# A chunked linear-attention layer and its MLP: v of the first three units loaded once and re-ordered by products, weights converted in five steps

## The chip, the cores and the metric

The kernel runs on one core of one Trainium2 chip. The metric is the device time of one execution in microseconds (us), as the median of several runs. Beside it there is one execution taken with the hardware profiler, whose span and rows are used below; it has a time of its own.

## The reference: what is computed

An attention block with a decaying state is followed by an MLP on its output.

```python
# B, H, S, D = 4, 8, 768, 48; q, k, v, f_logit are float32
f = 1 / (1 + exp(-f_logit))
state = zeros(B, H, D, D)
for t in range(S):
    state = f[:, :, t, :, None] * state + einsum('bhd,bhe->bhde', k[:, :, t], v[:, :, t])
    y[:, :, t] = einsum('bhd,bhde->bhe', q[:, :, t], state)
x = y.transpose(0, 2, 1, 3).reshape(3072, 384)
h = x @ w_in                          # w_in: 384 x 2048
g = h / (1 + exp(-1.702 * h))
out = g @ w_out                       # w_out: 2048 x 384
```

The two weight matrices arrive as float64 (6.3 MB each). The kernel reads them as pairs of 32-bit words and makes float32 of them itself.

## The kernel before, in words

**Units.** The 4 x 768 tokens are cut into 12 units of 256 tokens (three for each batch), numbered n = 0 to 11. A unit has an attention part, `attention(n)`, and an MLP part over its 256 rows. The first three units (`N_FILL = 3`) differ from the others in how q, k and f are brought in: they are loaded token-major (`load_raw`, L235) and turned by products with an identity matrix (`turn`, L311), copied out of PSUM by ScalarE (L314).

**Attention of a unit.** Within blocks of 64 tokens the work goes by levels m = 1, 2, 4, 8, 16, 32. At each level a "score" product `sc` (L349) is formed from the k of the first half and the q of the second half of each pair of blocks of m tokens; VectorE multiplies it by a mask (`evacuate`, L373) into A; and `add` (L406) multiplies A into the rows of v and adds into the PSUM tile `y`. Between two levels `promote` multiplies q and k by products of f: k on VectorE (L389), q on GpSimd (L390); ScalarE then copies the first halves of k into `Kc` (L396), which the next level's scores read. The tile `sc` has one buffer, so a level's scores also wait until the mask of the level before is through. After the levels, k is transposed (`tkn`, L467, copied to `kn` by ScalarE, L468), the products of k and v per block (L484) go into the running state `st` on VectorE (L498 to L503), and the state is multiplied into `y` (L519). ScalarE copies `y` out (L528), and DMAs re-arrange it into `xT`, the MLP's input (L530, L537).

**v in seven orders.** `add` needs the rows of v in seven orders: the even and the odd tokens of each pair (`vl` 0 and 1), and for each level m = 2 to 32 the first-half rows (`vl` 2 to 6). All are 128 x 384 tiles. A DMA first writes v of a unit token-major into a DRAM tile (`order_v`, L254: `v_tok`, in runs of 48 floats), then six DMAs read it back, one for orders 0 and 1 together (L267) and five for the others (L272), and a seventh reads it in plain token order (`load_vn`, L278) for L484. Each `vl` and `vn` has one buffer, so the loads for unit n + 1 wait until unit n has used the one before; they are issued at the levels of unit n.

**Weights.** `fetch_weights` (L160) brings the float64 weights as 16 pairs of pieces of 128 x 384; three buffers (`bits`) are in flight. For each piece ScalarE makes a float32 from the upper word (`a`, L188), and VectorE then runs a chain of six operations on 128 x 384 elements: L203 a maximum with a constant (the clamp), L204 shift and flip, L199 sign, L207, L208, L209. The operations of the two pieces of a pair alternate. `convert` issues one of them; `merge` spreads `pieces * NOP` such operations over the parts of a unit (8, 10, 8 and 6 pieces for units 0 to 3; NOP = 6), and MLP products over the same parts.

**Order.** The order of instructions on TensorE (PE) is written out by hand through all units, and on all engines up to unit 3: every engine then runs its list in that order. MLP products are laid in from unit 1 on; which of them may be issued depends on the pieces already converted. The SP queue issues nearly all DMAs in program order: first the q, k, f of unit 0, then weights, `vl` and `vn` of unit 0, then q, k, f of unit 1, and so on; only the first `v_tok` is issued by ScalarE. The program gives its DMAs eight completion counters in turn, so a DMA also waits until the one eight places before it has landed.

Of the kernel before, what the change touches and what calls it, by code (L numbers as in the profile page):

```python
# [23 lines left out]
def kernel(  # L24
# [40 lines left out]
    HS = 64  # L65
    LEV = [1 << i for i in range(C.bit_length() - 1)]
    NL = len(LEV)
# [43 lines left out]
    for l, m in enumerate(LEV):  # L111
        nc.vector.tensor_scalar(masks[:, l, :], at[0], float(m), None, op0=ALU.is_lt)

    F = const.tile([P, NA], F32, name="F")

    X = const.tile([P, 3, NA], F32, name="X")
# [23 lines left out]
                (lambda t: t[:], moe_w_out[ff * P:(ff + 2) * P, :].rearrange("(c p) f -> p c f", c=2))]))  # L140
        pieces += [w_in[:, :, ff * P:(ff + 1) * P] for ff in ffs] + [w_out[:, ff, :] for ff in ffs]
    NPC = 2 * FG
    NOP = 6
    fetched, todo = {}, []
    state = {"fetch": 0, "begin": 0, "done": 0}

# [20 lines left out]
    def begin_pair(m):  # L167

        chains = []
        for n in (2 * m, 2 * m + 1):
            if n not in fetched:
                continue
            dst = pieces[n]
            bits = fetched.pop(n)
            at = (slice(None),) * (len(dst.shape))
            lo, hi = bits[at + (0,)], bits[at + (1,)]

            def tmp(tag, bufs, n=n, dst=dst):  # L180
# [7 lines left out]
            nc.scalar.activation(a, hi.bitcast(F32), AF.Abs, scale=2.0 ** 112)  # L188
            chains.append(chain(dst, lo, hi, a, tmp))
        for ops in zip(*chains):  # L190
            todo.extend(ops)
        todo.append(None)

    def chain(dst, lo, hi, a, tmp):
        ve, ai, t = nc.vector, a.bitcast(I32), {}

        def sign():
            t["s"] = tmp("s", 2)
            ve.scalar_tensor_tensor(  # L199
                t["s"].bitcast(I32), hi, -(1 << 31), ai, op0=ALU.bitwise_and, op1=ALU.bitwise_or  # L200
            )
        return (
            lambda: ve.tensor_scalar(a, a, 2.0 ** 97, None, op0=ALU.max),  # L203
            lambda: ve.tensor_scalar(ai, ai, 3, -(1 << 31), op0=ALU.logical_shift_left, op1=ALU.bitwise_xor),  # L204
            sign,

            lambda: ve.tensor_scalar(ai, t["s"].bitcast(I32), -(1 << 23), None, op0=ALU.bitwise_and),  # L207
            lambda: ve.scalar_tensor_tensor(a, lo.bitcast(U32), 2.0 ** -52, a, op0=ALU.mult, op1=ALU.mult),  # L208
            lambda: ve.tensor_tensor(dst, a, t["s"], ALU.add),  # L209
        )  # L210
# [37 lines left out]

    def order_v(n, engine=nc.sync):

        if n >= NALL:
            return
        b, s0 = n // NU, n % NU * U
        engine.dma_start(  # L254
            out=v_toks[n % 2].rearrange("t (h d) -> t h d", h=H),
            in_=v[b, :, s0:s0 + U, :].rearrange("h t d -> t h d"),
        )

    def load_vl(n, u):


        if n >= NALL:
            return
        v_tok = v_toks[n % 2]
        if u == 0:
            t = ld.tile([P, 2, DM], F32, tag="vl0", name=f"vl_{n}_0")
            nc.sync.dma_start(out=t, in_=v_tok.rearrange("(p two) e -> p two e", two=2))  # L267
            vls[n, 0], vls[n, 1] = t[:, 0], t[:, 1]
        else:
            m, half = V_HALF[u]  # L270
            t = vls[n, u] = ld.tile([P, DM], F32, tag=f"vl{u}", name=f"vl_{n}_{u}")
            nc.sync.dma_start(out=t, in_=v_tok.rearrange("(n two m) e -> two n m e", two=2, m=m)[half])  # L272

    def load_vn(n):
        if n >= NALL:
            return
        vns[n] = ld.tile([P, NG, DM], F32, tag="vn", name=f"vn_{n}")
        nc.sync.dma_start(out=vns[n], in_=v_toks[n % 2].rearrange("(g p) e -> p g e", g=NG))  # L278

    def rows(h):  # L280
# [6 lines left out]
    def attention(n):  # L287
# [155 lines left out]
        def level(l):  # L443
            sc = scores()
            score(sc[:, :, :256].rearrange("p h (a t) -> p h a t", a=NP), keys(l), tokens(1, LEV[l], 1))
            if l == 2:
                add(1, slot(t["A"], 0), half(1, 1))
                add(2, slot(t["A"], 256), half(LEV[1], 1))
                load_vl(n + 1, 0)
                load_vl(n + 1, 2)  # L450
            else:
                add(l, slot(t["A"], 0), half(LEV[l - 1], 1))
                load_vl(n + 1, l)
            promote(l)
            t["A"] = evacuate(256, [(0, l)])

        for l in range(2, NL):
            part("W")(lambda l=l: level(l))
# [14 lines left out]
        @part("W")  # L473
        def _():
            add(NL, slot(t["A"], 0), half(LEV[-1], 1))
            load_vl(n + 1, NL)

            pd = scores()
            for a in range(NP):
                for g in range(NG):  # L480
                    for h in range(2):
                        for c in range(2):
                            x = (a * NG + g) * D
                            nc.tensor.matmul(  # L484
                                pd[h * HS:(h + 1) * HS, c, x:x + D],
                                lhsT=t["kn"][c * C:(c + 1) * C, a, g, h * HS:(h + 1) * HS],
                                rhs=vns[n][c * C:(c + 1) * C, g, (2 * a + h) * D:(2 * a + h + 1) * D],
                                start=True, stop=True,
                            )
            load_vn(n + 1)  # L490
            st = att.tile([P, NC, NP, D], F32, tag="st", name=f"st_{n}", bufs=2)
            D64 = t["tms"][NL].rearrange("p (a c) -> p a c", c=NC)
            prev = last.get("st")
            t["before"] = [prev[:, NC - 1] if c == 0 and not first else st[:, c - 1] if c else None for c in range(NC)]
            for c in range(NC):
                d = pd[:, c % 2, :NP * NG * D].rearrange("p (a g e) -> p a g e", a=NP, g=NG)[:, :, c // 2, :]
                if t["before"][c] is None:
                    nc.vector.tensor_copy(st[:, c], d)  # L498
                    continue
                nc.vector.tensor_tensor(  # L500
                    st[:, c], t["before"][c], D64[:, :, c:c + 1].broadcast_to((P, NP, D)), ALU.mult
                )
                nc.vector.tensor_tensor(st[:, c], st[:, c], d, ALU.add)  # L503
            last["st"] = st
# [80 lines left out]
    def mlp_unit(n):  # L585
        g = {}

        def done(tt, po):
            o = mlp.tile([P, DM], F32, tag="osb", name=f"osb_{n}_{tt}")
# [31 lines left out]
    def parts_of(n):  # L621

        parts = list(units[n][1])
        if n + 1 < NALL:
# [3 lines left out]
            parts.insert(9, ("-", begin_gates))  # L628
            parts.insert(8, ("B", begin_k))
            parts.insert(6, ("B", begin))  # L630
        return parts

    def merge(n, fill, columns, share, pieces=0, hold=0, by=1.0):
# [91 lines left out]
```

## Time and profile before

| | |
|---|---|
| median of 3 runs | 723.3 us (722.66 to 724.5) |
| profiled execution | 726.69 us, its span 724.9 us |
| mean granted TensorE clock | 0.974 |
| PE busy | 684.1 us (94% of the span) |
| VectorE (DVE) busy | 403.0 us (56%) |
| ScalarE (ACT) busy | 198.1 us (27%) |
| GpSimd (POOL) busy | 66.1 us (9%) |
| moved by DMA | 73.20 MB, mean 101 GB/s |

The profile's page gives busy times over the whole span; a matmul counts as busy from its start to its modelled end, so 94% is not 94% of the engine's peak. The span falls into two stages with different limits: the first hundred us or so, in which the weights come in and the first units run without much MLP work, and the long rest. Sums over the span say little about the first stage; it is read from tables by stretches of time, from the waits, and from the instructions in order of time. The 1.8 us between the span and the profiled time lie outside of the profiled instructions.

### The profile page before, as it was taken

How to read it: one execution, taken by the hardware profiler on the slowest of the kernel's cores; microseconds unless marked ns; L12 is line 12 of the kernel's file. 1: busy time of each engine (PE TensorE's matmuls, PEld its weight loads, DVE VectorE, ACT ScalarE, POOL GpSimd, SP SyncE). 2: the span in 40 equal slices, each digit the busy share in tenths (PEclk: the TensorE clock that was granted, in tenths of full speed). 3: DMA queues.
4: the chain of work that ended last, by engine and by line, in shares of the span. 5: the costliest groups of instructions: out<-in, count | busy, mean ns of one | idle time of the engine just before them, and what ended most of it. 6: DMA issues, size and time to landing. Idle time of an engine off the chain costs nothing.

```text
span 724.9 us, 20635 instructions
## 1 busy us (share of the span) xinstructions
PE 684.1 (94%) x9152; PEld 511.6 (71%) x9152; DVE 403.0 (56%) x697; ACT 198.1 (27%) x408; POOL 66.1 (9%) x103
## 2 busy tenths in 40 slices
PE   4567879999999999999999999999999999999998
PEld 4556657677677686686686686686686686686774
DVE  2959876798685753653653653653654654352120
ACT  2332442242222222222222222222222222122120
POOL 3314221210001001001001001001001001000000
PEclk9676999999999999999999999999999999999999
DMA  8879693385126434514513614514513211100000
GB/s 208 197 195 233 181 213 107 99 203 110 56 57 158 126 91 113 142 38 105 144 44 86 162 44 108 137 48 108 141 45 87 67 34 45 35 3 16 29 0 23
DMA packets 69097, 73.20 MB, mean 101 GB/s; under 512 B 30096, under 2 KB 61200, under 8 KB 69008
## 3 DMA queue, kind: packets, MB, share of 16 engines
q1 hardware_dynamic: 66944, 71.49, 38.4%
q8 instruction: 72, 1.18, 0.7%
q10 hardware_dynamic: 2064, 0.39, 0.3%
q14 instruction: 17, 0.14, 0.1%
HBM read 62.42 MB, written 9.44 MB: 99 GB/s over the span
## 4 chain that ended last, share of the span: by engine, by line
PE 86%; DVE 6%; DMA 5%; SPq 1%; issue 1%; ACT 1%; DVEq 0%; ACTq 0%
PE o L573 35%; PE h L557 33%; PE sc L349 6%; PE y L406 6%; PE sc L484 2%; DMA raw<-in_f_logit_dram 1%; PE y L519 1%; DMA v_tok<-in_v_dram 1%; PE tkn L467 1%; DMA bits<-in_moe_w_in_dram 1%; DMA bits<-in_moe_w_out_dram 1%; PE t L311 1%; DVE a L208 1%; DVE s L199 1%; DVE A L373 1%
## 5 line engine op out<-in xcount | busy, mean ns | idle before, releaser
L573 PE MATMUL o<-w_out,g 128*128 128x384 f32 x768 | 266.7, 496 | 2.8 <-DVE g L563 2.8
L557 PE MATMUL h<-xT,w_in 128*128 128x256 f32 x1152 | 264.3, 383 | 0.0
L557 PEld LDWEIGHTS h<-xT,w_in 128*128 128x128 f32 x1152 | 214.3, 190 | 33.3 <-issue 0.8
L573 PEld LDWEIGHTS o<-w_out,g 128*128 128x128 f32 x768 | 142.6, 191 | 94.8 <-issue 5.8
L563 DVE TENSOR_TENSOR g<-h,sg 128x256 f32<-128x256 f32 x192 | 80.9, 423 | 145.5 <-ACT sg L562 144.8
L562 ACT ACTIVATE sg<-h 128x256 f32<-128x256 f32 x192 | 73.5, 384 | 162.7 <-PE h L557 155.4
L396 ACT COPY Kc<-X 128x512 f32<-128x512 f32 x60 | 37.7, 629 | 171.9 <-DVE X L392 126.2
L392 DVE TENSOR_TENSOR X<-X,tot 128x1024 f32<-128x1024 f32 x45 | 54.9, 1219 | 35.2 <-PE sc L349 35.2
L373 DVE TENSOR_TENSOR A<-sc,masks 128x512 f32<-128x512 f32 (+1 forms) x84 | 62.6, 755 | 2.5 <-PE sc L349 2.5
L406 PE MATMUL y<-A,vl 64*48 64x64 f32 (+1 forms) x2688 | 61.9, 234 | 0.0
L406 PEld LDWEIGHTS y<-A,vl 64*48 64x48 f32 x2688 | 52.3, 125 | 5.8 <-issue 5.7
L349 PEld LDWEIGHTS sc<-X,Kc 48*64 48x64 f32 x1920 | 36.3, 142 | 28.2 <-issue 24.6
L338 POOL TENSOR_TENSOR tot<-F 128x512 f32<-128x512 f32 x12 | 12.5, 1041 | 479.2 <-DVE st L500 438.7
L349 PE MATMUL sc<-X,Kc 48*64 48x64 f32 x1920 | 44.1, 232 | 9.8 <-ACT Kc L396 8.1
L528 ACT COPY yT<-y 48x512 f32<-48x512 f32 x48 | 27.8, 580 | 76.1 <-PE y L519 57.9
L299 DVE STREAM_TRANSPOSE X<-raw 128x1024 f32<-128x1024 f32 x18 | 36.8, 2045 | 7.5 <-PE sc L349 7.1
L349 PEld LDWEIGHTS sc<-X 48*64 48x64 f32 x768 | 19.2, 144 | 22.9 <-issue 15.6
L349 PE MATMUL sc<-X 48*64 48x128 f32 (+1 forms) x768 | 24.0, 265 | 11.5 <-DVE A L373 5.6
L343 DVE TENSOR_TENSOR X<-X,F 128x1024 f32<-128x1024 f32 x12 | 14.7, 1223 | 25.3 <-PE y L519 15.5
L390 POOL TENSOR_TENSOR X<-X,tot 128x512 f32<-128x512 f32 x15 | 23.4, 1561 | 53.4 <-PE sc L349 53.4
L503 DVE TENSOR_TENSOR st<-st,sc 128x192 f32<-128x192 f32 x44 | 15.6, 354 | 19.9 <-PE sc L484 18.6
L392 DVE TENSOR_TENSOR X<-X,F 128x1024 f32<-128x1024 f32 x9 | 11.0, 1225 | 27.7 <-PE sc L349 27.7
(44 smaller groups left out, 365.0 us busy)
## 6 DMA issues: line engine op xcount, KB each, us to landing
vl<-v_tok SPq DMA_DIRECT2D x60, 192.0 KB
bits<-in_moe_w_out_dram SPq DMA_DIRECT2D x8, 768.0 KB
bits<-in_moe_w_in_dram SPq DMA_DIRECT2D x8, 576.0 KB
vl<-v_tok SPq DMA_DIRECT2D x12, 384.0 KB
vn<-v_tok SPq DMA_DIRECT2D x12, 384.0 KB
v_tok<-in_v_dram SPq DMA_DIRECT2D x11, 384.0 KB
xT<-yT SPq DMA_DIRECT2D x24, 144.0 KB
raw<-in_f_logit_dram SPq DMA_DIRECT2D x18, 192.0 KB
```

The lines of the kernel that those rows point to most:

```text
L299: nc.vector.transpose(out.rearrange("p (a i j) -> p a j i", a=NP, j=R), raw[:, j].rearrange("p a (j d) -> p (a j) d", j=R)[:, :, :32],)
L349: nc.tensor.matmul(out[g * HS:(g + 1) * HS, h, a, :], lhsT=lhs(h, a * U + g * G), rhs=rhs(h, a * U + g * G), start=True, stop=True,)
L373: nc.vector.tensor_tensor(A[:, :, c:c + w].rearrange("p h (x t) -> p h x t", t=64), t["sc"][:, :, c:c + w].rearrange("p h (x t) -> p h x t ...
L390: nc.gpsimd.tensor_tensor(qk[:, 0], qk[:, 0], by[:, 0], ALU.mult)
L392: nc.vector.tensor_tensor(qk, qk, by, ALU.mult)
L396: nc.scalar.copy(Kc.rearrange("p (n m) -> p n m", m=m), X[:, 2].rearrange("p (n two m) -> p n two m", two=2, m=m)[:, :, 0, :],)
L406: nc.tensor.matmul(dst(h, g, a), lhsT=vls[n, u][g * 64:(g + 1) * 64, (2 * a + h) * D:(2 * a + h + 1) * D], rhs=A(h, g, a), start=(start an ...
L528: nc.scalar.copy(yT[rows(h), :, g, :], py[columns(h, g), g])
L557: nc.tensor.matmul(ph, lhsT=w_in[:, c, ff * P:(ff + 1) * P], rhs=xTs[n][:, c, :], start=(c == 0), stop=(c == NK - 1))
L562: nc.scalar.activation(sg, ph, AF.Sigmoid, scale=1.702)
L563: nc.vector.tensor_tensor(g[ff // FG][:, ff % FG, :], ph, sg, ALU.mult)
L573: nc.tensor.matmul(t["po"], lhsT=g[ff // FG][:, ff % FG, tt * P:(tt + 1) * P], rhs=w_out[:, ff, :], start=(ff == ffs[0]), stop=(ff == ffs[ ...
```

## The change

For units 0, 1 and 2, v is loaded once in token order, straight from the input into `vn` (two DMAs of 128 tokens each, in runs of 48 floats); the DRAM tile and its six read-backs fall away for these units. The seven orders are made by products: for each order two products (g = 0, 1), with 64 columns of the identity, or of `perm`, as the stationary operand and the 128 x 384 rows of v as the moving one, fill the two halves of a PSUM tile, and ScalarE copies it to `vl`. `perm` holds identity columns for the levels 2 to 32, made once by five GpSimd copies. The products for unit 0 lie before and among its own first parts; those of unit n + 1 behind each level's `add` in unit n. `vn` of unit 1 takes the buffer of the MLP's output tile. That tile now holds both 128-row halves of a unit and has one buffer; before, each half had one of two.

The conversion of the weights loses the clamp (L203): ScalarE scales by 2 to the power -112 without taking the magnitude, VectorE shifts left by three without the flip, and the rest is as before. NOP goes from 6 to 5.

```diff
-    NOP = 6
+    NOP = 5
...
-            nc.scalar.activation(a, hi.bitcast(F32), AF.Abs, scale=2.0 ** 112)
+            nc.scalar.activation(a, hi.bitcast(F32), AF.Copy, scale=2.0 ** -112)
...
-            lambda: ve.tensor_scalar(a, a, 2.0 ** 97, None, op0=ALU.max),
-            lambda: ve.tensor_scalar(ai, ai, 3, -(1 << 31), op0=ALU.logical_shift_left, op1=ALU.bitwise_xor),
+            lambda: ve.tensor_scalar(ai, ai, 3, None, op0=ALU.logical_shift_left),
...
+    perm = const.tile([P, NL - 1, 64], F32, name="perm")
+    for u in range(2, NL + 1):
+        nc.gpsimd.tensor_copy(
+            perm[:, u - 2].rearrange("p (n m) -> p n m", m=LEV[u - 1]),
+            ident.rearrange("p (n two m) -> p two n m", two=2, m=LEV[u - 1])[:, 0],
+        )
...
     def order_v(n, engine=nc.sync):
-        if n >= NALL:
+        if n >= NALL or n < N_FILL:
             return
...
+        if n < N_FILL:
+            for i, x in enumerate((0, 1) if u == 0 else (u,)):
+                pt = ps.tile([P, DM], F32, tag="mm", name=f"tv_{n}_{x}", bufs=4)
+                for g in range(NG):
+                    nc.tensor.matmul(
+                        pt[g * 64:(g + 1) * 64], lhsT=ident[:, x::2] if u == 0 else perm[:, u - 2, :], rhs=vns[n][:, g, :],
+                        start=True, stop=True,
+                    )
+                if i == 0:
+                    t = ld.tile([P, 2, DM] if u == 0 else [P, DM], F32, tag=f"vl{u}", name=f"vl_{n}_{u}")
+                vls[n, x] = t[:, x] if u == 0 else t
+                nc.scalar.copy(vls[n, x], pt)
+            return
...
-        vns[n] = ld.tile([P, NG, DM], F32, tag="vn", name=f"vn_{n}")
+        vns[n] = (mlp if n == 1 else ld).tile([P, NG, DM], F32, tag="osb" if n == 1 else "vn", name=f"vn_{n}", bufs=1)
+        if n < N_FILL:
+            b, s0 = n // NU, n % NU * U
+            for g in range(NG):
+                nc.sync.dma_start(
+                    out=vns[n][:, g].rearrange("p (h d) -> p h d", h=H),
+                    in_=v[b, :, s0 + g * P:s0 + (g + 1) * P, :].rearrange("h p d -> p h d"),
+                )
+            return
...
     for j in range(3):
         load_raw(0, j)
-    order_v(0, nc.scalar)
+    load_vn(0)
     fetch_weights()
...
-    load_vl(0, 2)
-    load_vl(0, 3)
     fetch_weights()
-    for u in range(4, NV):
-        load_vl(0, u)
-    load_vn(0)
     for j in range(3):
         load_raw(1, j)
+    load_vn(1)
```

In the order written out, the products for `vl` 0 and 1 of unit 0 stand between the turning of q, k, f and the first scores; 2 and 3 behind the first scores; 4, 5 and 6 behind the second part's `add`. Those of unit 1 stand in unit 0: 0, 1 and 2 behind the `add` of level 2, then one order behind each `add`, and order 6 behind L484. Those of unit 2 stand in the same way in unit 1.

More of the change, by code (lines that the diff above doesn't have):

```diff
@@ L448, in level, with values @@
                 add(2, slot(t["A"], 256), half(LEV[1], 1))
-                load_vl(n + 1, 0)
-                load_vl(n + 1, 2)
             else:
                 add(l, slot(t["A"], 0), half(LEV[l - 1], 1))
-                load_vl(n + 1, l)
+            if n + 1 >= N_FILL:
+                values(l)
             promote(l)
             t["A"] = evacuate(256, [(0, l)])
+            if n + 1 < N_FILL:
+                values(l)
+        def values(l):
+            for u in (0, 2) if l == 2 else (l,):
+                load_vl(n + 1, u)
         for l in range(2, NL):
@@ L475, in _ @@
             add(NL, slot(t["A"], 0), half(LEV[-1], 1))
-            load_vl(n + 1, NL)
+            if n + 1 >= N_FILL:
+                load_vl(n + 1, NL)
             pd = scores()
@@ L489, in _ @@
                             )
-            load_vn(n + 1)
+            if n + 2 < N_FILL:
+                load_vn(n + 2)
+            if n + 1 >= N_FILL:
+                load_vn(n + 1)
+            else:
+                load_vl(n + 1, NL)
             st = att.tile([P, NC, NP, D], F32, tag="st", name=f"st_{n}", bufs=2)
@@ L588, in done @@
         def done(tt, po):
-            o = mlp.tile([P, DM], F32, tag="osb", name=f"osb_{n}_{tt}")
+            if tt == 0:
+                g["o"] = mlp.tile([P, U // P, DM], F32, tag="osb", name=f"osb_{n}", bufs=1)
+            o = g["o"][:, tt]
             nc.scalar.copy(o, po)
@@ L623, in parts_of @@
         parts = list(units[n][1])
+        if n == 0:
+            parts.insert(2, ("-", lambda: [load_vl(0, u) for u in range(4, NV)]))
+            parts.insert(1, ("-", lambda: [load_vl(0, u) for u in (2, 3)]))
         if n + 1 < NALL:
@@ L627, in parts_of @@
             parts.append((kind, lambda: (fn(), begin_q())))
-            parts.insert(9, ("-", begin_gates))
-            parts.insert(8, ("B", begin_k))
-            parts.insert(6, ("B", begin))
+            i = len(parts)
+            parts.insert(i - 1, ("-", begin_gates))
+            parts.insert(i - 2, ("B", begin_k))
+            parts.insert(i - 4, ("B", begin))
         return parts
```

## The prediction, as it was put on record

> **What bounds the kernel now.** I read the table of busy times by stretches first, since the share over the span hides two stages. Columns: stretch, its length, busy time of PE, PE weight loads, VectorE, ScalarE, GpSimd, granted clock, DMA share, GB/s.
>
> ```profile
> 14.60:36.00 21.40, 11.64 (x416) 10.45 (x416) 19.91 (x37) 5.92 (x12) 7.90 (x8) 0.73 0.86 206
> 36.00:49.80 13.80, 9.81 (x207) 8.94 (x200) 6.41 (x16) 5.33 (x10) 1.59 (x1) 0.87 0.84 212
> ...
> 56.70:80.00 23.30, 17.57 (x406) 14.51 (x410) 22.24 (x49) 6.60 (x15) 8.66 (x5) 0.79 0.85 221
> 80.00:94.00 14.00, 14.00 (x192) 10.54 (x191) 9.32 (x24) 6.90 (x13) 2.68 (x1) 0.90 0.82 187
> 94.00:107.00 13.00, 10.59 (x210) 7.83 (x200) 11.48 (x24) 4.35 (x9) 4.54 (x7) 1.00 0.95 214
> ...
> 155.00:200.00 45.00, 45.00 (x552) 32.29 (x551) 35.06 (x71) 13.32 (x29) 3.54 (x6) 1.00 0.45 108
> ```
>
> From about 110 us on PE is full and everything else is cover; what is gained there must be PE time, and the change gives none. Before that, in unit 0 (14.6 to 56.7) and unit 1 (56.7 to about 103), VectorE is the fullest: 19.9 of 21.4 us, 22.2 of 23.3. So the end moves by the time at which unit 2's dense part begins, and hardly by anything else.
>
> Second, the waits between 32 and 48 us, where VectorE has a hole (6.4 of 13.8 us):
>
> ```profile
> DVE a L203 <- ACT a L188: 5.2, 1, 5.2
> ACT a L188 <- DMA bits<-in_moe_w_out_dram: 4.8, 1, 4.8
> ...
> PE sc L484 <- ACT kn L468: 3.5, 1, 3.5
> ```
>
> ScalarE stood 4.8 us at the head of its list for a pair of weights, with `kn` behind it, and PE waited 3.5 us for `kn`. The SP queue in order of time says why these weights were late (start, length, instruction):
>
> ```profile
> 18.19 0.38 SPq L278 DMA_DIRECT2D vn<-v_tok  x1
> 19.07 4.85 SPq L235 DMA_DIRECT2D raw<-in_f_logit_dram  x4
> 24.62 4.83 SPq L235 DMA_DIRECT2D raw<-in_q_dram  x4
> 29.55 1.77 SPq L235 DMA_DIRECT2D raw<-in_k_dram  x4
> 31.37 0.65 SPq L254 DMA_DIRECT2D v_tok<-in_v_dram  x1
> 36.53 0.35 SPq L267 DMA_DIRECT2D vl<-v_tok  x1
> 36.98 0.57 SPq L272 DMA_DIRECT2D vl<-v_tok  x1
> 37.66 0.53 SPq L160 DMA_DIRECT2D bits<-in_moe_w_out_dram  x1
> ```
>
> Their DMA left at 37.66, behind unit 1's v, though their buffer was free at about 25, when the first pair's last L208 had run (23.69 + 1.02).
>
> **What the Trainium skill says.** "TensorE: Matmul & The Clock Gate", specifications: ScalarE and VectorE take instructions in strict order; the 4.8 us wait above, with `kn` behind it, agrees. Same page, part 3: products on different column groups of the array run side by side. The trace agrees: L311 writes 64 columns each, 64 products of 128 elements take 3.71 us at full clock (84.05), so 116 ns a pair, where one L557 of 256 takes 229 (264.3 us / 1152), so about 115 for 128. Same page, part 1: an idle PE is clocked at half speed until it has been busy some microseconds; the trace has 0.50 from 18 to 24 us and from 50 to 64. "DMA: Bandwidth & Descriptors", specifications: a transfer below 512 B is a read-modify-write. v's runs are 192 B; their cost into SBUF no row of before shows, into DRAM it does (below).
>
> **The change part by part**, against the profiled execution (726.7: span 724.9 and 1.8 outside), 3.4 above the median of 723.3.
>
> *1. Start: -1.3 us.* `v_tok`, at 0.73 beside the first loads, goes, and with it SP's 1.8 us wait for it in the middle of q. f should land about 1.3 earlier than 6.25 (0.39 MB less at 265 GB/s is 1.5). The turning of q, k, f keeps its 7.75 us on PE and ends near 12.7. The four products for `vl` 0 and 1 come next, two pairs of 384 elements: 3 x 116 = 0.35 us a pair warm, 0.48 cold (36 to 38 us: 25 in 2 us). They end at 13.4, about when ScalarE has copied k (12.7 + 0.6), so the first scores start at 13.4 against 14.69. The price rests on v's landing: issued at about 7.5, needed at 12.7. Bounds: `v_tok`'s queue moved 2064 packets in 0.3% of 16 engines' span, 2.2 us; at the mean of the main queue (38.4% x 16 x 724.9 / 66944 = 67 ns a packet) 2048 packets take 8.5; twice that, an estimate from the page's read-modify-write, is 17. I take 3 to 5 with latency.
>
> *2. Levels of unit 0: +0.5.* By level 5 the five-step chain issues 25 operations where the six-step one issued 30 (40 and 48 over 28 shares, 18 of them here). An L203 took 0.44 us (8.8 / 20 before 110 us), the operations left slightly more, so this is worth 4 to 5 x 0.4 = 1.8 where VectorE is the last to come. PE gets 11 pairs. A level has some 1.2 to 2 us in which PE waits for VectorE, GpSimd and `Kc`, which covers one pair, and two behind the first scores (PE idle 15.8 to 19.3). Not covered: orders 4 to 6, three cold pairs, 1.44 us; PE ends `add` at 21.6 and starts the scores at 23.1, where 22.91 was the old time, so the 1.3 and the first savings are gone; and of unit 1's orders 0 to 2 another 0.3. I charge 2.3. v of unit 1 must have landed by 26: SP now issues it at about 20, once the third pair of weights (3.9 MB from 2 us at 260 GB/s, near 17) has freed the counters. The seven ScalarE copies a unit (0.48 each, the duration of L605) are hidden: 5.9 busy of 21.4. The five `perm` copies fall in GpSimd's idle time from 2 to 10.6. Together 2.3 - 1.8 = +0.5, so -0.8 so far; bounds -1.8 and +3.
>
> *3. The wait for weights: -3.5.* The fourth pair is issued as soon as its buffer is free, near 25, and has 16 us to land. ScalarE copies `kn` at about 42, PE goes from `add` (ended 44.36) into L484, not at 47.83. Next late is the PE list itself, full from 36.05 to 44.36, with one pair more (in part 2). Sum -4.3.
>
> *4. Between state and unit 1: -0.4.* VectorE runs four instead of five chain operations (3.3 us from 52.03) before L343. -4.7.
>
> *5. Unit 1 to 84 us: -0.7.* 32 chain operations for 38 save 6 x 0.4 = 2.4. Against it ScalarE: its copies of `vl` stand before the sigmoids (L562) for which VectorE waits in order. At level 2 three copies (1.44) put `sg` at about 70.3 where VectorE gets to it at 69.5: 0.8; at level 3, where it waits 1.06 already, 0.5. From 80 to 94 PE is full: one pair, 0.35 to 0.4. 2.4 - 1.3 - 0.4 = 0.7. -5.4.
>
> *6. From 94 to 109.6: -0.9.* VectorE is the fullest again, and two to three L203 lie on the way to the `g` for which PE waits 2.8 us at 109.63. PE's list has one pair, under the state's 2.8 us. -6.3.
>
> *7. After that: +0.3.* The order of MLP products on PE is the same. The hole at 147.4 (1.63 us, PE behind VectorE) may shrink or grow by an operation; I leave +0.3 for it. Single-buffered output tile: its next user is a unit, some 45 us, later: nothing. Without the `v_tok` chain the weights also come earlier, but after 46 us nobody waited for them: nothing.
>
> Sum -6.0: 720.7 profiled, 717.3 as a median.
>
> **The rivals.**
>
> *A. The forecast, 717.3;* own range 714.8 to 720.5, the bounds of parts 2 and 5.
>
> *B. VectorE all the way.* If PE's pairs and ScalarE's copies are all covered, the 20 L203 before 110 us (8.8) and the hole of 4.8 both come back: 723.3 - 13.6 = 709.7. For it: 93 and 95% busy. Against: at 22.91 and 26.37 the scores already waited on PE's and GpSimd's side.
>
> *C. The pairs take the place of what goes.* 21 pairs at 0.42, the mean of warm and cold, are 8.8 us. If all are on the path in place of the 2.7 charged (2.3 and 0.4), the sum is -6.0 + 6.1: 723.4, no change. For it: PE is in order and every pair stands before scores. Against: PE is idle 9.8 of 21.4 us in unit 0.
>
> *D. Slower: v by token lands late.* With read-modify-write at 17 us, v of unit 0 lands at 24.5 and PE, in order, starts the first scores at 25.2, 10.5 after before. Parts 2 to 7 (-4.7) stay: 723.3 + 5.8 = 729.1. It decides from a landing later than 12.7 + 6 = 18.7 on. For it: 2048 runs of 192 B, ahead of the weights in the same queue. Against: `v_tok` had the same runs, and its first load took 5.2 us in the chain of waits.
>
> That the change doesn't do what it says could only be the ScalarE step: Copy for magnitude. L314 uses Copy already and the page has a single table load, so I give it no price.
>
> **How the numbers follow.** A 0.50, B 0.12, C 0.20, D 0.18. A measurement of this kernel tells 0.3%, 2.2 us, from no change: below 721.1 is faster, above 725.5 slower. A and B are faster (0.62), C is spread over 720 to 726 and gives 0.03 faster, 0.13 same, 0.04 slower; D gives 0.02 same and 0.16 slower. Faster 0.65, same 0.15, slower 0.20. The range of 710.0 to 725.5 leaves out most of D and some of B, about 0.2.
>
> **What would show it right or wrong.** Right: first scores near 13.4; ScalarE's wait for `bits` near 42 gone and L484 near 43.5; unit 1's first scores at 52; PE dense from about 103.5; the rest shifted by the same. Part 2 is wrong if the scores behind orders 4 to 6 start much past 23; part 5 if VectorE waits more than 2.5 us for `sg`. D shows as PE waiting for `vn`, C as PE full in unit 0 with VectorE in holes.

## The result and the profile after

The changed kernel takes 729.48 us (median of 4 runs, 728.03 to 731.29) beside 723.9 us of the kernel before (4 runs, 722.66 to 724.55): a ratio of 1.008 with a 95% interval of [1.0053, 1.0108], so slower by half a per cent to one. A second set of runs, 21 of the changed kernel beside 74 of the one before, gave 728.79 us and 1.0042 [1.0025, 1.0059]. The forecast of 717.3 us was wrong in its sign. The two profiled executions stand closer than the medians: 728.03 us (span 726.1) against 726.69 (span 724.9). The one of before lies 2.8 us above its median, the one of the changed kernel 1.5 below. A trace is one execution; where ratios and traces differ in size below, the ratios decide.

First comes the table by stretches of the changed kernel, with the columns of the prediction (stretch, length, busy PE, weight loads, VectorE, ScalarE, GpSimd, granted clock, DMA share, GB/s):

```profile
14.60:36.00 21.40, 15.83 (x358) 9.52 (x356) 15.17 (x25) 8.82 (x19) 5.27 (x5) 0.84 0.63 162
36.00:49.80 13.80, 11.68 (x245) 9.57 (x248) 10.48 (x20) 7.03 (x14) 2.03 (x2) 0.88 0.48 118
...
56.70:80.00 23.30, 19.04 (x397) 14.31 (x398) 21.13 (x37) 6.67 (x15) 7.09 (x6) 0.79 0.29 86
80.00:94.00 14.00, 13.04 (x178) 9.19 (x178) 11.74 (x27) 7.83 (x16) 1.06 (x1) 1.00 0.66 153
94.00:107.00 13.00, 11.38 (x235) 8.64 (x232) 9.39 (x21) 6.20 (x13) 3.88 (x7) 1.00 0.96 225
```

In the first stretch the busy time of VectorE, the fullest engine before (19.91 us), is down to 15.17, and that of PE is up from 11.64 to 15.83. The hole of VectorE in the second stretch is filled (6.41 to 10.48). The DMA share fell from 0.86 to 0.63 and from 0.84 to 0.48. So the wait for weights and the transfers have gone, but a new hole of VectorE has opened one stretch earlier. The list of waits of the changed kernel from 16 to 36 us says what it waits for (engine, line, releaser: us in total, times, longest):

```profile
DVE A L403 <- PE sc L379: 6.1, 1, 6.1
...
PE tv L277 <- DMA vn<-in_v_dram: 3.5, 1, 3.5
```

VectorE stands 6.1 us before a mask, for scores that PE hasn't made yet, and PE stands 3.5 us before a product for `vl` whose v hasn't landed. PE's instructions in order of time tell which v it is:

```profile
18.71 1.90 PE L436 MATMUL y<-A,vl 64*48 64x128 f32 x32
20.54 2.97 PE L277 MATMUL tv<-vn,perm 128*64 128x384 f32 x12
23.44 0.69 PE L379 MATMUL sc<-X,Kc 48*64 48x64 f32 x32
23.96 1.08 PE L436 MATMUL y<-A,vl 64*48 64x64 f32 x64
28.52 2.77 PE L277 MATMUL tv<-vn,ident 128*64 128x384 f32 x7 [3.48 <-DMA vn<-in_v_dram]
...
31.28 1.62 PE L277 MATMUL tv<-vn,perm 128*64 128x384 f32 x3
32.83 0.69 PE L379 MATMUL sc<-X,Kc 48*64 48x64 f32 x32
```

At 20.54 are unit 0's orders 4 to 6. At 28.52 begin unit 1's orders 0, 1 and 2, for which nothing in unit 0 waits. But PE takes its list in order, and unit 0's scores of level 3 stand behind them: they start at 32.83, against 26.37 before. The chain of waits (start, length, what) goes back from there to a pair of weights,

```profile
9.81 11.14 DMA bits<-in_moe_w_out_dram
...
24.27 4.21 DMA vn<-in_v_dram
28.47 0.04 issue
28.52 4.39 PE tv L277 x12
```

and the SP queue of the changed kernel shows how that pair holds v up:

```profile
9.81 0.55 SPq L169 DMA_DIRECT2D bits<-in_moe_w_out_dram  x1
10.46 3.19 SPq L243 DMA_DIRECT2D raw<-in_f_logit_dram  x4
14.22 7.06 SPq L243 DMA_DIRECT2D raw<-in_q_dram  x4
21.38 2.85 SPq L243 DMA_DIRECT2D raw<-in_k_dram  x4
24.27 1.05 SPq L303 DMA_DIRECT2D vn<-in_v_dram  x2
25.43 0.84 SPq L169 DMA_DIRECT2D bits<-in_moe_w_out_dram  x1
```

The four q loads of unit 1 take 7.06 us to issue. SP's own list of waits from 6 to 30 us has 5.2 us for `w_in`, part of it at the last f load, and 2.6 for `w_out`: eight places before the last of the q loads stands the third pair of weights, whose completion counter it needs. That pair landed at 20.97; v was issued at 24.27 and landed at 28.48.

The table follows the delay through the two traces (start of the first instruction of each kind, in us; L484 of before is L520 of after):

| | before | after | difference |
|---|---|---|---|
| unit 0, first scores | 14.69 | 13.15 | -1.5 |
| unit 0, scores of level 3 | 26.37 | 32.83 | +6.5 |
| unit 1, turning of q, k, f | 36.05 | 41.91 | +5.9 |
| unit 0, state product | 47.83 | 49.30 | +1.5 |
| unit 1, first scores | 56.71 | 57.54 | +0.8 |
| unit 1, second scores | 60.86 | 62.94 | +2.1 |
| unit 2, turning | 84.05 | 86.13 | +2.1 |
| unit 2, first scores | 103.10 | 105.07 | +2.0 |
| PE dense from | 109.63 | 111.45 | +1.8 |

### The profile page after: what moved, and what is told of

It reads as the page before. It is cut to its first block, busy times and chain, and to the rows that moved or that the text cites. A ratio compares the mean times of both kernels' runs of the same rounds, so it can differ in the third digit from the quotient of the medians.

```text
span 726.1 us, 20759 instructions
## 1 busy us (share of the span) xinstructions
PE 695.9 (96%) x9236; PEld 512.4 (71%) x9236; DVE 399.6 (55%) x665; ACT 207.0 (29%) x429; POOL 62.2 (9%) x108
## 4 chain that ended last, share of the span: by engine, by line
PE 90%; DVE 4%; DMA 2%; SPq 2%; issue 1%; ACT 1%; DVEq 0%; ACTq 0%
PE o L614 35%; PE h L598 34%; PE sc L379 7%; PE y L436 6%; PE y L560 2%; PE t L341 2%; DMA bits<-in_moe_w_out_dram 2%; PE sc L520 2%; PE tkn L502 1%; PE tv L277 1%; SPq L243 1%; DMA vn<-in_v_dram 1%; DVE s L208 0%; DVE a L215 0%; DVE w_in L217 0%
## 5 line engine op out<-in xcount | busy, mean ns | idle before, releaser
L436 PEld LDWEIGHTS y<-A,vl 64*48 64x48 f32 x2688 | 51.3, 122 | 5.8 <-issue 5.7
L379 PEld LDWEIGHTS sc<-X,Kc 48*64 48x64 f32 x1920 | 34.4, 136 | 23.3 <-issue 21.3
L379 PE MATMUL sc<-X,Kc 48*64 48x64 f32 x1920 | 42.0, 225 | 3.2 <-ACT Kc L426 3.1
L368 POOL TENSOR_TENSOR tot<-tot 128x256 f32<-128x256 f32 (+4 forms) x60 | 24.2, 403 | 4.7
```

The costliest lines, as they stand in the source:

```text
L368: nc.gpsimd.tensor_tensor(tn, t2[:, :, 0], t2[:, :, 1], ALU.mult)
L379: nc.tensor.matmul(out[g * HS:(g + 1) * HS, h, a, :], lhsT=lhs(h, a * U + g * G), rhs=rhs(h, a * U + g * G), start=True, stop=True,)
L436: nc.tensor.matmul(dst(h, g, a), lhsT=vls[n, u][g * 64:(g + 1) * 64, (2 * a + h) * D:(2 * a + h + 1) * D], rhs=A(h, g, a), start=(start an ...
```

## The experiments

The theory is that PE's list stands behind unit 1's v, and that the change would gain without that. There are two rivals: the products themselves cost PE what is lost, or the shorter chain, laid in differently (NOP 5), does. Each kernel's ratio is to the kernel before in runs on the same chip. "Before" in a heading means that the edit is made to the kernel before, "changed" that it is made to the changed kernel. The diffs are cut to the lines that matter; "..." marks what is left out.

**The shorter chain alone: before with the change's conversion.**

```diff
-    NOP = 6
+    NOP = 5
...
-            nc.scalar.activation(a, hi.bitcast(F32), AF.Abs, scale=2.0 ** 112)
+            nc.scalar.activation(a, hi.bitcast(F32), AF.Copy, scale=2.0 ** -112)
...
-            lambda: ve.tensor_scalar(a, a, 2.0 ** 97, None, op0=ALU.max),
-            lambda: ve.tensor_scalar(ai, ai, 3, -(1 << 31), op0=ALU.logical_shift_left, op1=ALU.bitwise_xor),
+            lambda: ve.tensor_scalar(ai, ai, 3, None, op0=ALU.logical_shift_left),
```

> The kernel before with the weights' part of the change alone: five steps instead of six, NOP 5. Theory (v by products is the loss; the shorter chain is a gain where VectorE is fullest): 1 to 3 us below before, so 721 to 723. Rival (the new order of the chain among the other work costs more than it saves, since VectorE's busy time in the changed kernel fell by only 3.4 us where 13.6 us of L203 went): same as before or up to 3 us above.

723.53 us, 0.9986 [0.997, 1.0001]: a gain of 1 us, two at most, or nothing. The chain does no harm, and gains far less than the 5.5 us (1.8, 0.4, 2.4 and 0.9) that parts 2, 4, 5 and 6 gave it.

**The products alone: changed with the six-step chain** (the same edit the other way round).

> The changed kernel with the old six-step chain, NOP 6. Theory (v is the loss): as slow as the changed kernel or 1 to 3 us slower, 729 to 733. Rival (the chain is the loss): near or below before, 720 to 724.

728.97 us, 1.005 [1.0036, 1.0064]. So the part that concerns v alone gives the whole slowdown. The wait is in this kernel's list too, from 14 to 36 us:

```profile
PE tv L278 <- DMA vn<-in_v_dram: 3.6, 1, 3.6
```

**v of unit 1 loaded early: changed with its load directly behind unit 0's.**

```diff
     load_vn(0)
+    load_vn(1)
     fetch_weights()
...
     for j in range(3):
         load_raw(1, j)
-    load_vn(1)
```

> The changed kernel with v of unit 1 loaded directly behind v of unit 0, ahead of the weights and of unit 1's q, k, f. Theory (PE stands 3.5 us for unit 1's v, and the cold products behind the wait make it 6.4 us late): the wait goes, the first scores of level 3 start near 27 instead of 32.8, and the end is 3 to 6 us earlier than the changed kernel, 724 to 726.5. Rival (the wait is only the form that the delay takes; the products themselves, at twice the price that I charged, are the loss): at most 1.5 us earlier, 728 to 729.5.

722.02 us, 0.9962 [0.9945, 0.9979]: with this one load moved, the kernel is faster than before. No wait for `vn` is left; the level 3 scores start at 28.4, unit 0's state product at 43.44, unit 1's first scores at 51.69.

**Products of unit 1 issued later: changed with orders 0 to 3 behind unit 0's state product and 4 to 6 behind unit 1's first scores**, v loaded where the change loads it.

```diff
+            if n == 1:
+                for u in (4, 5, 6):
+                    load_vl(n, u)
...
-            if n + 1 < N_FILL:
+            if n + 1 < N_FILL and n:
...
-                load_vl(n + 1, NL)
+                for u in (0, 2, 3) if n == 0 else (NL,):
+                    load_vl(n + 1, u)
```

> The changed kernel with unit 1's products moved out of unit 0's levels: orders 0 to 3 behind L520 of unit 0, orders 4 to 6 behind the first scores of unit 1; same number of products. Theory (unit 0's levels are where the loss arises): level 3 of unit 0 starts near 25, unit 1's first scores at 53 to 55 instead of 57.5, the end 2 to 5 us earlier than the changed kernel. Rival (price of the products, wherever they stand): unit 1's first scores come 1 to 2 us after the state instead, and the end is within 1.5 us of the changed kernel.

721.35 us, 0.9945 [0.9922, 0.9967]. Level 3 starts at 25.8, earlier than the 26.37 of before, and the state product at 42.44. The load of unit 1's v is issued as late as in the changed kernel (24.40 beside 24.27) and costs nothing, because nothing urgent stands behind it. Two cures of opposite kind, one at the load and one at the list, take away the same loss.

**The changed kernel again**, beside the next four.

> The changed kernel once more, as the yardstick beside the next three on the same chip, and for a second profile. Theory (PE waits for unit 1's v, a DMA whose time varies): ratio to before 1.004 to 1.010, and a wait of PE for vn of 3 us or more between 24 and 32 us, perhaps longer than the 3.5 us of the first profile. Rival (the loss is in the number of products, which doesn't vary): the same ratio with a wait under 2 us.

728.79 us, 1.0042 [1.0025, 1.0059], with a wait of 3.6 us for `vn` and level 3 at 33.08. Against it the two cures are worth 0.0080 and 0.0097 of 725: 5.8 and 7.0 us, give or take 2, as the ratios come from two sets of runs.

The time at which unit 0's first scores start varies by about a us from one execution to the next. The stretch from there to unit 0's scores of level 3 varies less. It takes 11.7 us before, 19.7 and 19.0 in the two traces of the changed kernel, 14.5 with v early, and 12.4 with the products late. So the wait and what hangs on it cost some 5 us there, and the products of unit 1 another 2.

**Both cures at once.**

> Both: v of unit 1 loaded behind that of unit 0, and its products moved out of unit 0's levels. Theory (both cure the same thing, products in front of unit 0's level 3 that are not ready): no more than 1 us better than the better one of the two, ratio to before 0.993 to 0.996. Rival (two separate losses, a late DMA and full PE slots in the levels): the gains add, ratio 0.988 or less.

722.77 us, 0.9962 [0.9948, 0.9976]: they don't add, so both cure the same thing.

**Each product issued twice, on top of the early load.** It adds 21 pairs of products to PE's work and changes no result.

```diff
-                for g in range(NG):
+                for g in (0, 1, 0, 1):
```

> The kernel with v of unit 1 loaded early, and each of the 42 products for the orders of v issued twice (the second writes the same values again). By the trace a pair takes 0.72 us at full clock, so PE gets 15 us more. Theory (with v there in time most of the products lie in time in which PE would wait for VectorE): 4 to 8 us over the early kernel. Rival (the price of the products is on the path): 12 to 16 us over it.

728.36 us, 1.0038 [1.0023, 1.0053]. Against the early load that is 0.0076 x 725 = 5.5 us for 21 pairs, again give or take 2. A pair takes 0.70 us or more at full clock (below), so the 21 are some 15 us of PE, and about a third of it is on the path. If the first set costs as much as the second, which no run shows, the products cost 5.5 us where I had charged 2.7. So the products are a cost in their own right, but not the cause of the sign: with that cost in it, the early load is still faster than before.

**Products for unit 0 only**: units 1 and 2 get v through the DRAM tile as before.

```diff
+    N_VP = 1
...
-        if n >= NALL or n < N_FILL:
+        if n >= NALL or n < N_VP:
...
-        if n < N_FILL:
+        if n < N_VP:
```

(and so at each other place that asks for these units.)

> The changed kernel with products only for unit 0's v; units 1 and 2 get theirs over the DRAM tile, as before. Theory (unit 1's v in front of unit 0's level 3 is the loss; the wait of ScalarE for the fourth pair of weights comes back, behind unit 1's v): no PE wait near 28 us, a wait for weights of 2 to 5 us near 42, and a ratio to before of 0.995 to 1.001. Rival (the start, with unit 0's own products, is already a loss): 1.003 or more.

721.3 us, 0.9945 [0.9931, 0.9958]: as good as the best so far, with a third of the products. The wait for weights that I expected back (2 to 5 us) did not come: VectorE's wait for ScalarE's `a` is 0.2 us (5.2 before). With unit 0's `v_tok` and read-backs out of the queue, the fourth pair leaves at 29.28 instead of 37.66. Unit 1's first scores start at 51.49 and unit 2's at 96.73, in a profiled execution that was 3 us faster than this kernel's median.

**Unit 0 only, with orders 4, 5 and 6 one behind each of three adds** in place of together at 20.5.

> Products for unit 0 alone, and its orders 4, 5 and 6 one behind each of three adds instead of all three behind the second part's add, where they took 3.4 us before level 2 in the kernel with products for unit 0 alone. Theory (at twice the price that I charged they are on the path there; one pair a level fits the idle time of PE): level 2 starts 1 to 2 us earlier, and the ratio to before is 0.002 to 0.003 lower than 0.9945. Rival (VectorE is the fullest, so PE's place is cover anyway): no change, 0.9935 to 0.9955.

721.6 us, 0.9941 [0.9923, 0.996]. Level 2 does start 1.1 us earlier (22.87 instead of 23.94), as expected, but level 3 already starts later (26.75 instead of 26.02), and nothing is left of it at the end.

**Unit 0 only, with the six-step chain.**

> Products for unit 0 alone with the old six-step chain, NOP 6. Theory (the shorter chain pays where no wait stands in front of it; alone it gave 1 us, since the wait for the fourth weights swallowed the rest): ratio 0.998 to 1.000, that is 3 to 4 us above the same kernel with five steps. Rival (the chain is worth 1 us anywhere): 0.9955 to 0.9965.

720.47 us, 0.9929 [0.9908, 0.9949]. I had thought that the shorter chain pays once the waits are gone. It doesn't: the ratio lies below what either theory or rival gave, its interval overlaps that of the five-step form, and the median is the lower one. This is the fastest kernel of the study by its median, though the two others with products for unit 0 only and the one with late products can't be told from it.

**The weights' wait alone: before with unit 1's first v transfers moved behind the fourth pair of weights.** It should have the gain of part 3, and has no product for `vl` at all.

```diff
-            order_v(n + 1)
+            if n:
+                order_v(n + 1)
...
-                load_vl(n + 1, 0)
-                load_vl(n + 1, 2)
+                if n:
+                    load_vl(n + 1, 0)
+                    load_vl(n + 1, 2)
...
+                if n == 0 and l == 3:
+                    order_v(1)
+                    load_vl(1, 0)
+                    load_vl(1, 2)
```

> The kernel before with one change of order on the SP queue: the DMA of the fourth pair of weights ahead of unit 1's v. Theory (part 3 of the prediction: ScalarE's wait of 4.8 us costs 3.5): L484 of unit 0 at 44 to 45 instead of 47.8, the end 2.5 to 3.5 us earlier, ratio 0.995 to 0.997. Rival (the wait hides time that VectorE needs anyway for its list, and comes back later): ratio 0.999 to 1.001.

724.27 us, 0.9987 [0.9971, 1.0003]: close to what the rival gave (0.999 to 1.001); the theory's range lies outside the interval. At its place part 3 is right: the state product is at 42.72 (5.1 earlier than before) and unit 1's first scores at 51.25 (5.5 earlier). At unit 2's first scores, 102.67, only 0.4 of it is left. The waits of this kernel from 60 to 112 us show where it went, and its SP queue shows why:

```profile
DVE g L569 <- ACT sg L568: 6.0, 3, 4.5
...
PE h L563 <- DMA xT<-yT: 2.3, 1, 2.3
```

```profile
54.41 1.78 SPq L235 DMA_DIRECT2D raw<-in_k_dram  x4
56.30 0.57 SPq L272 DMA_DIRECT2D vl<-v_tok  x1
57.38 0.39 SPq L278 DMA_DIRECT2D vn<-v_tok  x1
58.58 0.60 SPq L536 DMA_DIRECT2D xT<-yT  x1
```

ScalarE had copied `yT` by 49.0. But its transfer to `xT` stands in the same queue behind unit 2's q, k, f and unit 1's last v, and left at 58.58, only 0.5 earlier than before.

**The same, with unit 2's q, k, f behind `xT`**, to test that reading.

```diff
-                load_raw(n + 1, 0)
-                load_raw(n + 1, 1)
+                if n != 1:
+                    load_raw(n + 1, 0)
+                if n != 1:
+                    load_raw(n + 1, 1)
...
-                load_raw(n + 1, 2)
+                if n != 1:
+                    load_raw(n + 1, 2)
...
+            if n == 0:
+                for j in range(3):
+                    load_raw(2, j)
```

> The kernel before with the fourth pair of weights ahead of unit 1's v in the SP queue (as in the experiment before it, ratio 0.9987), and with the loads of unit 2's q, k and f moved behind unit 0's xT, which stood behind them in that queue (issued at 58.6 though yT was copied by 49). Theory, that the gain of 5 us at the state product was given back to the wait for xT: xT issued near 51, PE's wait of 2.3 us for xT and most of VectorE's 6.0 us for sg gone, first scores of unit 2 below 100 (102.7 there), ratio about 0.994 to 0.996. Rival, that PE and VectorE are full in unit 1 whatever comes first: xT earlier, but the first scores of unit 2 stay at 102 or later and the ratio stays at 0.998 to 1.000. If the raw tiles of unit 2 come late instead, PE waits for raw before its turn (81 there) and nothing is gained either.

723.18 us, 0.998 [0.9964, 0.9996]. The first half of the theory came true: `xT` leaves at 48.79 and PE no longer waits for it (its first h product is at 61.92 instead of 65.11). The ratio is the rival's, and unit 2's first scores, at 101.27, lie between the two. Neither had the reason, which stands in this kernel's ScalarE and SP lists:

```profile
71.11 0.97 ACT L188 ACTIVATE a<-bits 128x384 f32<-128x384 f32 x2 [2.71 <-DMA bits<-in_moe_w_out_dram]
```

```profile
64.84 1.84 SPq L235 DMA_DIRECT2D raw<-in_k_dram  x4
66.79 0.38 SPq L160 DMA_DIRECT2D bits<-in_moe_w_out_dram  x1
```

The next pair of weights now stands behind q, k and f, ScalarE waits 2.7 us for it, and VectorE 3.8 us for the `sg` behind that: the wait of part 3 again, a unit later. In the kernel with products for unit 0 only, which moves less through this queue, the same pair left at 53.44 instead of 66.79, and unit 2's first scores came at 96.73. That this is what is left of the loss is a reading of the two traces; no run separates it.

All of them stand in one table. The last three columns (us) are from a single profiled execution, which can lie up to 3 us off its kernel's median; the two of the changed kernel differ by 0.8 and 1.1 us in the first scores. From unit 2's first scores to the end of the profiled time it is 621.5 to 623.6 us in all 14 of them, so what sets these executions apart lies almost all before that point.

| kernel | us | ratio | profiled, us | unit 1, unit 2, first scores | wait for `vn` |
|---|---|---|---|---|---|
| before | 723.9 to 725.6 | 1 | 726.69 | 56.7, 103.1 | |
| changed | 729.48 | 1.008 [1.0053, 1.0108] | 728.03 | 57.5, 105.1 | 3.5 |
| changed again | 728.79 | 1.0042 [1.0025, 1.0059] | 729.41 | 58.3, 106.2 | 3.6 |
| chain alone | 723.53 | 0.9986 [0.997, 1.0001] | 724.09 | 55.7, 100.9 | |
| products alone | 728.97 | 1.005 [1.0036, 1.0064] | 725.88 | 56.7, 103.9 | 3.6 |
| v of unit 1 early | 722.02 | 0.9962 [0.9945, 0.9979] | 722.61 | 51.7, 99.4 | none |
| its products late | 721.35 | 0.9945 [0.9922, 0.9967] | 721.45 | 50.6, 98.5 | none |
| early and late | 722.77 | 0.9962 [0.9948, 0.9976] | 722.13 | 53.2, 100.6 | none |
| early, products twice | 728.36 | 1.0038 [1.0023, 1.0053] | 726.99 | 54.0, 105.3 | none |
| unit 0 only | 721.3 | 0.9945 [0.9931, 0.9958] | 718.26 | 51.5, 96.7 | none |
| the same, spread | 721.6 | 0.9941 [0.9923, 0.996] | 721.8 | 53.4, 100.3 | none |
| the same, six steps | 720.47 | 0.9929 [0.9908, 0.9949] | 722.31 | 52.8, 100.3 | none |
| weights first | 724.27 | 0.9987 [0.9971, 1.0003] | 725.39 | 51.3, 102.7 | |
| weights, then `xT` | 723.18 | 0.998 [0.9964, 0.9996] | 724.79 | 51.6, 101.3 | |

## Why the prediction was wrong, point by point

*What bounds the kernel:* half right. That the end moves by the time at which unit 2 gets going held in all 14 traces (621.5 to 623.6 us from its first scores on). VectorE was the fullest engine before that, but the order of the loads in the one SP queue matters as much in the first two units: three different waits for it (weights, `xT`, weights again) came up one behind the other in the last two experiments.

In the traces of before and of the first changed run, parts 1 to 5 measure -1.54, +7.40, -4.39, -0.64 and +1.25 us, and 6 and 7 together -0.86. They add up to the +1.2 between the two spans. The medians are 3 to 5.6 us apart; on which part the rest falls is open.

*1. Start, -1.3:* the direction is right, the nearness in part luck. The first scores start at 13.15 (13.4 put), 1.5 earlier than before. Two errors cancelled in this: the turning began at 4.51 instead of near 4.95 and ended 0.8 earlier than put, and the two pairs of products took 1.4 us (11.75 to 13.15) instead of 0.7. Nor is -1.5 a firm figure. Three more traces with the old start have the first scores at 13.55 to 14.11, and the second trace of the changed kernel has them at 14.04. v of unit 0 was issued at 6.34 and nobody waited for it; its turn came at 11.75.

*2. Levels of unit 0, +0.5:* **this step failed**, and gave the sign. From the start to the turning of unit 1 the difference went from -1.5 to +5.9, so it cost 7.4 us in this trace (6.2 in the second) where +0.5 was put. Two terms of it were wrong.

The first is the arrival of unit 1's v. I had written: "v of unit 1 must have landed by 26: SP now issues it at about 20, once the third pair of weights (3.9 MB from 2 us at 260 GB/s, near 17) has freed the counters". The third pair landed at 20.97. The queue moved 237 GB/s from 2 us to there, not 260, and by then it had moved 4.5 MB, since unit 1's f and part of its q went along. v was issued 3.3 us later, because the last q load and the four of k still stood before it, and it landed at 28.48 instead of by 26. I gave this need no price for being missed, although a late v holds up unit 0's own scores. Curing it, at either end, is worth 5.8 to 7.0 us.

The second is the price of a pair of products: I read 64 records of L311 as 64 products. For the 42 products of `tv` the changed kernel's trace holds 84 records (60 with `perm`, 24 with `ident`): a float32 product leaves two. My comparison with L557 had the same error in it (1152 records, 576 products) and so agreed; that a pair takes no longer than one such product still holds. Two pairs at full clock take 1.40 us (11.75 to 13.15), 0.70 each and not 0.35, and three at a mean clock of 0.71 take 2.90 (20.54 to 23.44), not 1.44. Unit 1's orders 0 to 2, for which I charged 0.3, took 4.4 us (28.52 to 32.90): PE had stood idle before them, and the granted clock was 0.61 in the mean and 0.50 from 30 to 32 us.

*3. The wait for weights, -3.5:* right at its place, and a little more. From the turning of unit 1 to the state product the difference falls from +5.9 to +1.5, ScalarE's wait of 4.8 us is gone, and the 5.1 us of the experiment with the weights alone say the same. But on its own this gain brought the end forward by only 0.9 us, and by the interval perhaps not at all: what is won must find `xT` and the next weights ready.

*4. Between state and unit 1, -0.4:* the difference fell by 0.6 in the trace, about as put.

*5. Unit 1, -0.7:* wrong, +1.3. ScalarE's order was priced well: VectorE waits 2.1 us for `sg` in two places, where 1.3 on top of 1.06 was expected. A term that I had put at nothing is the orders 0 to 2 of unit 2. PE has no gap there, so these three pairs push the scores of level 3 from +1.7 to +3.6 (72.65 beside 69.04):

```profile
68.15 1.51 PE L277 MATMUL tv<-vn,ident 128*64 128x384 f32 x8
69.49 0.81 PE L277 MATMUL tv<-vn,perm 128*64 128x384 f32 x4
70.24 2.48 PE L598 MATMUL h<-xT,w_in 128*128 128x256 f32 x10
```

Of the chain's 2.4 at most the 1.5 came by which the difference shrinks from there to the turning of unit 2. And 1.3 us came in at a place where nothing was changed: the promotion of k before the second scores took three times as long. First comes the instruction in the changed kernel, with GpSimd's half of the promotion, then the same in the kernel before:

```profile
59.63 1.49 POOL L420 TENSOR_TENSOR X<-X,F 128x512 f32<-128x512 f32 x1 [2.16 <-DVE w_out L217]
```

```profile
59.65 2.01 DVE L419 TENSOR_TENSOR X<-X,F 128x512 f32<-128x512 f32 x1
```

```profile
58.79 2.15 POOL L390 TENSOR_TENSOR X<-X,F 128x512 f32<-128x512 f32 x1 [3.31 <-PE sc L349]
```

```profile
58.90 0.68 DVE L389 TENSOR_TENSOR X<-X,F 128x512 f32<-128x512 f32 x1
```

VectorE's instruction ends 0.54 us after GpSimd's half has ended (61.66 and 61.12), and that is a pattern. Of the 252 promotions of k by this instruction in the 14 traces 48 took 1.5 us or more, and each of these began while GpSimd's half was running and ended 0.54 or 0.55 us after it; the others took about 0.68. As these rows read, VectorE stood until GpSimd was through; no run takes the two apart. Where GpSimd's half is the long one, as before, it may have been the one to stand. The trace of the chain alone has 2.01 us at this place too, and that of the products alone 0.68, so v is not needed for it. But the six-step kernel with products for unit 0 only has 1.97, so the shorter chain is not needed either, and why the lot falls on one engine or the other is open.

*6 and 7, -0.9 and +0.3:* -0.3 to the dense part and -0.6 after it. Together near what was put.

*The chain's term across parts 2, 4, 5 and 6* (5.5 us) was too large everywhere: 1.0 us alone, with an interval that reaches 0; nothing that can be told in the changed kernel (1.0042 against 1.005, intervals overlapping); and nothing for unit 0 only. VectorE's groups say why part of it never existed. The first block is of before, the second of after (busy us, mean ns of one):

```profile
L199 DVE SCALAR_TENSOR_TENSOR s<-bits,a 128x384 int32<-128x384 int32 x32 | 17.8, 582 | 0.0
...
L203 DVE TENSOR_SCALAR a<-a 128x384 f32<-128x384 f32 x32 | 13.6, 444 | 5.3 <-ACT a L188 5.2
L204 DVE TENSOR_SCALAR a<-a 128x384 int32<-128x384 int32 x32 | 12.0, 397 | 0.0
```

```profile
L208 DVE SCALAR_TENSOR_TENSOR s<-bits,a 128x384 int32<-128x384 int32 x32 | 19.5, 630 | 0.0
...
L212 DVE TENSOR_SCALAR a<-a 128x384 int32<-128x384 int32 x32 | 13.8, 446 | 1.1 <-ACT a L197 1.0
```

L199 of before is L208 of after, and L204 is L212. With 13.6 us of L203 taken out, VectorE's busy time fell by only 3.4 us, from 403.0 to 399.6, and the operations left (L208, L212 and others) grew. Two things are in this. An L203 took 350 ns in the median, 444 in the mean and 1121 at the most: the mean holds a few long ones. In both traces all operations of the chain that were lengthened by 0.3 us or more ran beside a GpSimd instruction that had begun before them, like the promotion above, so this time stays when L203 goes and falls on a neighbour. And the records of operations that follow each other overlap:

```profile
27.12 0.61 DVE L203 TENSOR_SCALAR a<-a 128x384 f32<-128x384 f32 x2
27.66 0.35 DVE L204 TENSOR_SCALAR a<-a 128x384 int32<-128x384 int32 x1
```

Two undisturbed L203 hold the next one up for 0.54 us, 0.27 each, where I had put 0.4. And how much of VectorE's busy time lay on the path I had not shown.

*The rivals.* D had the mechanism (PE in order, behind a v that lands late, to be seen as PE waiting for `vn`), but at unit 0's v, which was in time. I had looked at the first load of v and not at the second, which stands behind three pairs of weights and the twelve loads of q, k and f. That D's 729.1 comes so near is luck: it is a delay of 10.5 us less gains of 4.7, and the runs show neither of the two. C was of the right kind: doubling the products showed 5.5 us for 21 pairs. But its 8.8 us, for all of them on the path, rest on the halved price; at 0.70 a pair that would be some 15. B is out: with the wait for unit 1's v cured, the kernels stand at 720.5 to 722.8, far from its 709.7, and the 8.8 us of L203 in it were counted at the mean of 0.44.

*What stays open:* which of the four kernels at 0.993 to 0.9945 is the best; whether the shorter chain is worth 1 us or nothing; and whether the two ratios of the changed kernel (1.008 from four runs, 1.0042) differ at all, as their intervals just overlap.

## What to carry to other kernels

Work that is moved onto an engine that runs its list in order brings its data's arrival time along. For each moved instruction ask when its operand lands, at the measured rate of that stretch and behind everything queued before it, and who stands behind the instruction if it is late. Prepare the next unit's data behind the present unit's critical instructions, or load it first; either cured the loss here. A wait that is taken off a shared queue was worth at the end only what the next load in that queue let through. And price an operation in a busy list by the time from its start to the next one's start where nothing disturbs it (0.27 us here), not by its mean duration (0.44).

## What the runs showed that was not expected

- A float32 product leaves two matmul records: 84 for 42 products. Two products of 64 columns and 384 elements together took 0.70 us at full clock (three such pairs from 68.15 to 70.24).
- Four loads of 96 KB took 7.06 us to issue behind a pair of weights that took 11.14 us to land; with v of unit 1 loaded before the weights, the same q loads took 7.29 us.
- Two loads of v in runs of 192 B landed 4.21 us after the first was issued, amid weights; "DMA: Bandwidth & Descriptors" of the Trainium skill (specifications) calls transfers below 512 B read-modify-writes. No row shows one, and the bound of 17 us that I had estimated from it was far too high.
- PE, after 3.5 us of waiting, took 4.4 us for three pairs of products, at a mean clock of 0.61; three pairs of unit 2 at full clock took 2.1 us.
- In 48 of 252 promotions VectorE's instruction took 1.5 to 2.0 us instead of 0.68. It had begun while GpSimd's half was running, and ended 0.54 or 0.55 us after it, in every one of the 48.
